# Attention and channel-mixing kernel: wider score banks, the mean read from its bank, the sums of P by two copies

## The chip, the cores and the metric

The kernel runs on one core of a Trainium2 chip. The metric is the device time of one execution in microseconds (us); every figure "ns" or "us" below comes from the times or the profile of this kernel. Engines: TensorE (PE in the profile; PEld is its weight load), VectorE (DVE), ScalarE (ACT), GpSimd (POOL), SyncE (SP, which issues most DMAs).

## The reference, cut to what matters

```python
# q, k, v: (8, 8, 576, 64); s: (8, 8, 576)
scores = (q @ k.T) / sqrt(64)
cum = cumsum(maximum(s, 0))
bias = -(cum[..., :, None] - cum[..., None, :])
scores = where(causal, -1e9, scores + minimum(bias, 0))
scores = scores - max(scores)
attn = exp(scores); attn = attn / (sum(attn) + 1e-9)
x = (attn @ v), heads side by side            # (8, 576, 512)
mixed = real(fft(fft(x, axis=1), axis=2))
u = x + mixed
un = (u - mean(u)) / sqrt(mean((u - mean(u))**2) + 1e-6)
out = u + maximum(un @ w_ch1, 0) @ w_ch2      # 512 -> 2048 -> 512
```

## The kernel before, in words

The 64 heads are worked in 32 pairs (`pair`, two heads side by side on the partitions), four pairs to a batch; after each batch its Fourier transform runs as matmuls (`folds`, `fourier`); after the attention comes the two-layer network over nine tiles of 512 tokens. Of the network, the first two tiles and the weights' conversion are woven into the end of the attention and the last Fourier transform (`norm_flow`, `plain_flow`, `mlp`); the third tile's norm is also made by `norm_flow`; the other tiles run in `fast_tile` with `ln_tile`, at an even pace to the end.

For one pair: `high` and `low` round q and k and make the rests, `maxes` finds the largest score of each query (units of matmuls into "psm" banks, reduced on VectorE), `scores` makes P, `av` makes P times v and the sums of P, `copies` takes those out, `recip` and `finish` divide.

`scores`, for each head: the keys stand in five chunks `CH` of 128, 128, 128, 128 and 64 keys, each against the queries that may see it. Chunk 0 takes two banks of 256 and 320 columns, chunk 1 one of 448, chunk 2 one of 320, chunk 3 one of 256 (of which 192 are used) and chunk 4 one of 64: six banks of 512 columns at most, from a ring of three ("ps") that the Fourier transform and the network's first product also use. Each bank gets two matmuls, one of KQ by KQ (L684) and one of K1 by Q1 for the rests (L685), each with its own 128x128 weights, and then one exponential on ScalarE (L690) that writes P in SBUF. When the exponentials of chunks 0 to 3 are done, one GpSimd instruction (`select`, L709) clears the triangle of four blocks; chunk 4 has one of its own (L697). `av` waits for both.

`av` puts the sums of P (one32 as the weights, L748) into the same bank as the first 128 columns of P times v (L740): sums of queries 0 to 383 on partitions 0 to 63, columns 0 to 383, sums of queries 384 to 575 on partitions 64 to 127, columns 0 to 191, values in columns 384 to 511. `copies` takes them out by three ScalarE instructions: 64x384 and 64x192 with the bias tile `tiny` (1e-9) added (L772), and 128x128 (L776). Two DMAs then gather the sums to a 48x24 tile, `recip` takes the reciprocal on VectorE (L789) and sends it through DRAM to all partitions (rd, rb), and `finish` multiplies (L820, L824).

`norm_flow`, for the first three tiles: the mean comes out of a matmul with `ones` into a bank; ScalarE copies it to SBUF (L1197); VectorE subtracts it from the four quarters of u (L1202); ScalarE squares the quarters (L1209, L1212) and GpSimd adds the squares (L1214); a second matmul, a root (L1223) and a reciprocal (L1226) follow. The quarters without their mean are rounded on ScalarE (L1235), VectorE makes the rests (L1238), and the product with w_ch1 (L1396) needs them.

The order of the instructions on each engine is not left to a scheduler of the compiler. `Flow` plays the program through with a cost for each step and due times built from the numbers in `PR`, and emits the instructions in the order in which it places them; an engine then works through its list in that order. A change of a cost or of a number in `PR` can change the order on every engine up to the end of this part, at some 700 us.

## Time and profile before

| | us |
|---|---|
| median of 3 runs | 1318.52 (1315.52 to 1319.11) |
| profiled execution, its own time | 1313.49 |
| its span in the trace | 1311.8 |
| granted TensorE clock, mean over the span | 0.982 of full |

| engine | busy share of the span |
|---|---|
| TensorE, matmuls | 94% |
| TensorE, weight loads | 79% |
| VectorE | 59% |
| ScalarE | 46% |
| GpSimd | 42% |

The profiled execution lies 5.0 us under the median. A busy TensorE in the profile counts a matmul until its modelled end, so neighbouring matmuls overlap in it: its pace is read from the starts of consecutive matmuls. The row of a wait names the engine that was idle and what it had waited for.

### The profile page before, as it was taken

Reading aid. Unit: us, or ns where it says so; the run is one execution under the profiler, and the core shown is the slowest. Engines: PE = TensorE matmul, PEld = TensorE weight load, DVE = VectorE, ACT = ScalarE, POOL = GpSimd, SP = SyncE. Lnnn points to the kernel's source line nnn. Section 1 sums busy time; section 2 is a strip of 40 time slices with the busy share of each in tenths; the row PEclk is TensorE's granted clock in tenths of the full one; section 3 lists DMA queues with packets and bytes.
Section 4 is the critical chain, followed back from the end, with each engine's and each line's share of the span. In section 5 each row is a group of like instructions: output and inputs, shape, how many; then the busy total and the mean of one; then the engine's idle time right before and its main releaser. Section 6 shows DMA issues by size and latency. Waiting matters only on the chain.

```text
span 1311.8 us, 22882 instructions
## 1 busy us (share of the span) xinstructions
PE 1235.9 (94%) x8414; PEld 1031.7 (79%) x8414; DVE 780.0 (59%) x1440; ACT 607.2 (46%) x1388; POOL 551.0 (42%) x569
## 2 busy tenths in 40 slices
PE   3998889899999979899999999999999999999998
PEld 2766667677776757787788888899888988888987
DVE  6566776847678577839757865444454444535323
ACT  2876776667676563425333432333233333333221
POOL 9456676857758675528743502102021021120100
PEclk9999899999999999999999999999999999999999
DMA  8867675646666465277543335244353442533433
GB/s 192 226 183 208 179 204 171 196 118 182 175 167 175 107 210 196 76 245 233 185 152 130 114 121 174 96 145 151 103 173 119 137 154 96 171 118 122 147 102 113
DMA packets 120395, 205.61 MB, mean 157 GB/s; under 512 B 16537, under 2 KB 38457, under 8 KB 120283
## 3 DMA queue, kind: packets, MB, share of 16 engines
q1 hardware_dynamic: 117707, 200.96, 49.1%
q0 software_dynamic: 1712, 2.53, 1.1%
q8 instruction: 66, 1.08, 0.3%
q10 hardware_dynamic: 864, 0.67, 0.2%
q14 instruction: 46, 0.38, 0.1%
HBM read 148.44 MB, written 31.72 MB: 137 GB/s over the span
## 4 chain that ended last, share of the span: by engine, by line
PE 55%; DVE 8%; POOL 3%; issue 3%; DMA 2%; ACT 1%; SPq 0%; POOLq 0%; DVEq 0%; ACTq 0%
PE b L347 20%; PE acc L259 7%; PE acc L258 7%; PE acc L260 7%; PE h L1396 4%; DVE we L88 1%; PE acc L1378 1%; PE acc L1377 1%; PE acc L1379 1%; DVE we L85 1%; PE pav L733 1%; PE pz L926 1%; DVE wl L1087 1%; PE pav L748 1%; DMA w2l<-wD 1%
## 5 line engine op out<-in xcount | busy, mean ns | idle before, releaser
L305 POOL TENSOR_TENSOR w<-w,o 128x512 f32<-128x512 f32 x28 | 37.2, 1338 | 346.5 <-DVE o L301 307.0
L259 PE MATMUL acc<-zh,w2l 128*128 128x512 f32 x452 | 179.3, 397 | 0.0
L258 PE MATMUL acc<-zh,w2h 128*128 128x512 f32 x452 | 178.8, 396 | 0.0
L260 PE MATMUL acc<-zl,w2h 128*128 128x512 f32 x452 | 177.2, 392 | 0.0
L690 ACT ACTIVATE P<-ps 128x320 f32<-128x320 f32 (+4 forms) x384 | 130.1, 393 | 41.3 <-PE ps L685 35.1
L684 PE MATMUL ps<-KQ 128*128 128x256 f32 (+3 forms) x384 | 121.9, 330 | 6.9 <-ACT P L690 6.3
L339 ACT ACTIVATE zh<-cs 128x256 fp32r<-128x256 f32 x112 | 58.8, 525 | 141.6 <-DVE cs L359 86.0
L685 PE MATMUL ps<-Q,K 128*128 128x256 f32 (+3 forms) x384 | 114.9, 312 | 0.0
L340 DVE SCALAR_TENSOR_TENSOR zl<-cs,zh 128x256 fp32r<-128x256 f32 x112 | 66.0, 590 | 69.2 <-ACT zh L339 69.2
L603 DVE CUSTOM_DVE_ANT_0 trash<-pm,amask 128x384 bf16<-128x384 f32 (+1 forms) x128 | 79.1, 618 | 39.4 <-PE pm L600 33.0
L554 POOL TENSOR_TENSOR Q<-qk,Q 64x576 fp32r<-64x576 f32 x64 | 95.2, 1508 | 17.1 <-DMA Q<-KQ 7.5
L347 PEld LDWEIGHTS b<-bh,wh 128*128 128x128 f32 x448 | 83.8, 188 | 22.0 <-DVE cs L359 2.4
L260 PEld LDWEIGHTS acc<-zl,w2h 128*128 128x128 f32 x452 | 85.0, 188 | 19.3 <-DVE zl L340 0.4
L347 PE MATMUL b<-bh,wh 128*128 128x256 f32 x448 | 89.2, 280 | 1.6 <-DVE cs L359 1.6
L684 PEld LDWEIGHTS ps<-KQ 128*128 128x128 f32 x384 | 75.4, 196 | 19.0 <-ACT P L690 14.2
L347 PE MATMUL b<-bh,wl 128*128 128x256 f32 x448 | 90.0, 282 | 0.0
L347 PE MATMUL b<-bl,wh 128*128 128x256 f32 x448 | 89.6, 281 | 0.0
L259 PEld LDWEIGHTS acc<-zh,w2l 128*128 128x128 f32 x452 | 86.3, 191 | 2.6
L733 PE MATMUL pav<-P,va 128*64 128x448 f32 (+3 forms) x640 | 87.3, 419 | 0.0
L258 PEld LDWEIGHTS acc<-zh,w2h 128*128 128x128 f32 x452 | 84.8, 188 | 2.9
L359 DVE TENSOR_TENSOR cs<-cs,b 128x256 f32<-128x256 f32 x56 | 23.5, 420 | 103.9 <-PE b L347 103.2
L733 PEld LDWEIGHTS pav<-P,va 128*64 128x64 f32 x640 | 43.2, 137 | 49.0 <-issue 39.8
(223 smaller groups left out, 3114.3 us busy)
## 6 DMA issues: line engine op xcount, KB each, us to landing
w2h<-w2D SPq DMA_DIRECT2D x128, 256.0 KB
w2l<-w2D SPq DMA_DIRECT2D x128, 256.0 KB
qk<-in_qkT_dram SPq DMA_DIRECT2D x32, 576.0 KB
raw<-in_wP_dram SPq DMA_DIRECT2D x32, 512.0 KB
va<-in_vA_dram SPq DMA_DIRECT2D x32, 320.0 KB
u<-uD SPq DMA_DIRECT2D x10, 1024.0 KB
Q<-KQ SPq DMA_DIRECT2D x32, 288.0 KB
K<-KQ SPq DMA_DIRECT2D x32, 288.0 KB
```

What stands on the lines that cost most here:

```text
L258: nc.tensor.matmul(acc[j], a[:, cs], y, start=first, stop=False)
L259: nc.tensor.matmul(acc[j], b[:, cs], y, start=False, stop=False)
L260: nc.tensor.matmul(acc[j], a[:, cs], z, start=False, stop=final)
L339: nc.scalar.activation(y[0][:, at], src, AF.Relu)
L340: nc.vector.scalar_tensor_tensor(out=y[1][:, at], in0=src, scalar=0.0, in1=y[0][:, at].bitcast(F32), op0=ALU.max, op1=ALU.subtract)
L347: nc.tensor.matmul(p[:, 0:256], a[:, j * 128:(j + 1) * 128], b[:, j], start=start and i == 0, stop=i == 5, skip_group_check=not start)
L554: nc.gpsimd.tensor_sub(q1[64:128, h], qk[0:64, h], q1[0:64, h].bitcast(F32))
L603: nc.vector.tensor_tensor_reduce(out=trash[:, 0:n], in0=p[:, 0:n], in1=amask[:, m0:m0 + n], scale=1.0, scalar=NEG, op0=ALU.add, op1=ALU.ma ...
L684: nc.tensor.matmul(p[:, :n], ky[:, h, ksl], qy[:, h, a:a + n], start=True, stop=False)
L685: nc.tensor.matmul(p[:, :n], k1[:, h, ksl], q1[:, h, a:a + n], start=False, stop=True)
L690: nc.scalar.activation(P[:, o:o + a + n - lo], p[:, lo - a:n], AF.Exp, scale=0.125)
L733: nc.tensor.matmul(p[64 * h:64 * h + 64, 0:n], va[:, c, 64 * h:64 * h + 64], P[h][:, o:o + n], start=start, stop=stop)
```

## The change

Four things change in what the kernel does, and the numbers in `PR` with them.

1. Scores take four banks a head: chunk 0's first 512 columns; its last 64 with chunk 1's 448; chunk 2's 320; chunk 3's 192 with chunk 4's 64. In a bank with two pieces there are four matmuls, so there are still twelve to a head. There is one exponential to a bank, and `select` waits for all four.
2. The first unit of `maxes` computes 128 columns a head and not 256.
3. The sums of queries 384 to 575 go to columns 192 to 383 of their bank; two ScalarE copies of 128x320 and 64x192 take sums and values out, without `tiny`; the 1e-9 is added on VectorE ahead of the reciprocal.
4. In `norm_flow` the mean is not copied: VectorE subtracts it from its bank; the squares are added on VectorE.

Of the numbers in `PR` nearly all are other ones; among them `T` goes from 14.85 to 14.86, `sel` 7.33 to 5.72, `av` 10.36 to 12.41, `lw` 41.24 to 50.68, `kp` 22.34 to 7.87, `dw` 8.84 to 4.43, `c0` 22.43 to 26.95, `fo2` 37.01 to 40.62, `fo3` 43.31 to 47.59.

```diff
-    tiny = const.tile([128, 1], F32, name="tiny")
-    nc.gpsimd.memset(tiny, 1e-9)
...
+            n = 256 if cut is None else cut + 128
...
-                nc.tensor.matmul(both[:, h], qy[:, h, 128 * c:128 * c + 128], ky[:, h, k0:k0 + 256], start=not h, stop=cut is None and h == 1, skip_group_check=True)
+                nc.tensor.matmul(both[:, h, 0:n], qy[:, h, 128 * c:128 * c + 128], ky[:, h, k0:k0 + n], start=not h, stop=cut is None and h == 1, skip_group_check=True)
...
-            def one(h, c, a, n, P, diag):
-                nk, q0, nq, qk = CH[c]
-                ksl = slice(128 * c, 128 * c + 128)
-                e, hold = yield pe(2 * mm(max(n, 128)), ring=(ring("ps", 3), 1))
+            def one(h, parts, P, diag):
+                total = sum(n for _, _, n in parts)
+                e, hold = yield pe(2 * sum(max(0.075, mm(n)) for _, _, n in parts), ring=(ring("ps", 3), 1))
                 p = bank("ps")
-                nc.tensor.matmul(p[:, :n], ky[:, h, ksl], qy[:, h, a:a + n], start=True, stop=False)
-                nc.tensor.matmul(p[:, :n], k1[:, h, ksl], q1[:, h, a:a + n], start=False, stop=True)
+                for x, (kk, qq) in enumerate(((ky, qy), (k1, q1))):
+                    o = 0
+                    for y, (c, a, n) in enumerate(parts):
+                        nc.tensor.matmul(p[:, o:o + n], kk[:, h, 128 * c:128 * c + 128], qq[:, h, a:a + n], start=x == y == 0, stop=x == 1, skip_group_check=True)
+                        o += n
...
-                e = yield act(a + n - lo, e)
-                nc.scalar.activation(P[:, o:o + a + n - lo], p[:, lo - a:n], AF.Exp, scale=0.125)
+                e = yield act(total, e)
+                nc.scalar.activation(P[:, o:o + total], p[:, 0:total], AF.Exp, scale=0.125)
...
+            for x, parts in enumerate((((0, 0, 512),), ((0, 512, 64), (1, 128, 448)), ((2, 256, 320),), ((3, 384, 192), (4, 512, 64)))):
+                flow.add(one(h, parts, P, diag), D(i) + PR['sc'] + PR['sch'] * h + PR['scs'] * 1.5 * x)
...
-                    nc.tensor.matmul(p[r:r + 32, a - 384 * t:a - 384 * t + n], one32, P[h][:, o:o + n], start=False, stop=k == 4, skip_group_check=True)
+                    nc.tensor.matmul(p[r:r + 32, a - 192 * t:a - 192 * t + n], one32, P[h][:, o:o + n], start=False, stop=k == 4, skip_group_check=True)
...
-            nc.scalar.activation(x[64 * t:64 * t + 64, 0:n], p[64 * t:64 * t + 64, 0:n], AF.Identity, bias=tiny[64 * t:64 * t + 64])
...
-        nc.scalar.copy(x[:, 384:512], p[:, 384:512])
+        nc.scalar.copy(x[:, 192:512], p[:, 192:512])
...
+        nc.scalar.copy(x[0:64, 0:192], p[0:64, 0:192])
...
+        nc.vector.tensor_scalar(sums, sums, 1e-9, None, op0=ALU.add)
         nc.vector.reciprocal(sums, sums)
...
-        mu, hmu = yield from tmp("mu")
-        e = yield act(512, e)
-        nc.scalar.copy(mu, pm)
...
-            nc.vector.tensor_sub(u[:, j], u[:, j], mu)
+            nc.vector.tensor_sub(u[:, j], u[:, j], pm)
...
-            e = yield pool_(512, e)
-            nc.gpsimd.tensor_add(t, t, t2)
+            e = yield dve(512, e)
+            nc.vector.tensor_add(t, t, t2)
```

## Rows read from the trace of the kernel before

**Rows 1.** The busy time of each engine by stage: stretch in us from the span's start, then busy us and instructions of TensorE, its weight loads, VectorE, ScalarE and GpSimd, the granted TensorE clock, the DMA engines' busy share and GB/s.

```profile
core 0: us, PE busy (x) PEld busy (x) DVE busy (x) ACT busy (x) POOL busy (x), PEclk, DMA share, GB/s
32.00:460.00 428.00, 401.34 (x3564) 306.53 (x3565) 296.14 (x664) 302.71 (x739) 291.14 (x329) 0.97 0.63 177
480.00:500.00 20.00, 11.24 (x51) 9.10 (x50) 20.00 (x28) 12.97 (x25) 15.86 (x9) 0.81 0.62 211
520.00:540.00 20.00, 16.17 (x83) 13.48 (x81) 19.98 (x27) 12.31 (x26) 11.94 (x10) 1.00 0.53 171
600.00:620.00 20.00, 16.90 (x65) 13.10 (x65) 18.66 (x18) 11.05 (x21) 16.59 (x12) 0.91 0.88 292
680.00:700.00 20.00, 20.00 (x88) 16.22 (x87) 10.32 (x13) 6.72 (x13) 5.48 (x4) 1.00 0.31 105
760.00:1311.00 551.00, 545.41 (x3384) 489.44 (x3382) 247.93 (x449) 170.75 (x388) 65.20 (x50) 1.00 0.40 132
```

**Rows 2.** Who waited for whom between 40 and 472 us, by engine: the idle engine, the tile and line that waited, what it waited for, the total in us, how often, the longest.

```profile
PEld ps L684 <- ACT P L690: 13.8, 31, 2.0
PEld pav L740 <- POOL P L709: 7.5, 13, 0.9
PEld pm L600 <- DVE Mx L593: 5.4, 7, 2.8
ACT P L690 <- PE ps L685: 33.8, 60, 1.7
POOL P L709 <- ACT P L690: 12.7, 9, 3.3
POOL xr L824 <- DMA rb<-rd: 11.4, 5, 6.3
```

**Rows 3.** TensorE's matmuls in order of time within 250 to 256 us: start, duration, line, operation, shape.

```profile
251.06 0.28 PE L685 MATMUL ps<-Q,K 128*128 128x256 f32 x1
251.18 0.31 PE L684 MATMUL ps<-KQ 128*128 128x320 f32 x1
251.33 0.31 PE L685 MATMUL ps<-Q,K 128*128 128x320 f32 x1
251.47 0.36 PE L684 MATMUL ps<-KQ 128*128 128x448 f32 x1
251.68 0.37 PE L685 MATMUL ps<-Q,K 128*128 128x448 f32 x1
251.88 0.35 PE L684 MATMUL ps<-KQ 128*128 128x320 f32 x1
...
254.65 0.28 PE L685 MATMUL ps<-Q,K 128*128 128x256 f32 x1
254.76 0.20 PE L684 MATMUL ps<-KQ 128*128 128x64 f32 x1
254.79 0.28 PE L685 MATMUL ps<-Q,K 128*128 128x64 f32 x1
```

**Rows 4.** TensorE's weight loads in order of time, same stretch and columns.

```profile
250.83 0.19 PEld L684 LDWEIGHTS ps<-KQ 128*128 128x128 f32 x1
250.94 0.19 PEld L685 LDWEIGHTS ps<-Q,K 128*128 128x128 f32 x1
251.06 0.19 PEld L684 LDWEIGHTS ps<-KQ 128*128 128x128 f32 x1
251.18 0.19 PEld L685 LDWEIGHTS ps<-Q,K 128*128 128x128 f32 x1
251.33 0.19 PEld L684 LDWEIGHTS ps<-KQ 128*128 128x128 f32 x1
...
254.65 0.19 PEld L684 LDWEIGHTS ps<-KQ 128*128 128x128 f32 x1
254.77 0.19 PEld L685 LDWEIGHTS ps<-Q,K 128*128 128x128 f32 x1
```

**Rows 5.** Groups of ScalarE instructions between 32 and 472 us, shapes kept apart: line, operation, out<-in, shape, count, then busy us and mean ns of one, then the engine's idle time before them and what ended it.

```profile
L690 ACT ACTIVATE P<-ps 128x320 f32<-128x320 f32 x128 | 56.0, 437 | 12.9 <-PE ps L685 10.9 <-ACT mt L649 1.7
L690 ACT ACTIVATE P<-ps 128x448 f32<-128x448 f32 x64 | 34.9, 545 | 5.9 <-PE ps L685 5.6
L690 ACT ACTIVATE P<-ps 128x256 f32<-128x256 f32 x64 | 24.6, 385 | 10.3 <-PE ps L685 8.5 <-PE pm L600 0.9
L690 ACT ACTIVATE P<-ps 128x192 f32<-128x192 f32 x64 | 21.2, 331 | 7.3 <-PE ps L685 6.4 <-PE pm L624 0.8
L772 ACT ACTIVATE stage<-pav,tiny 64x384 f32<-64x384 f32 x31 | 17.8, 575 | 24.1 <-PE pav L748 19.2 <-POOL P L709 2.5 <-issue 1.3
L763 ACT COPY stage<-pav 128x448 f32<-128x448 f32 x31 | 16.4, 530 | 11.5 <-PE pav L733 11.2
L690 ACT ACTIVATE P<-ps 128x64 f32<-128x64 f32 x64 | 14.3, 224 | 5.0 <-PE ps L685 3.8 <-PE pm L600 0.8
L772 ACT ACTIVATE stage<-pav,tiny 64x192 f32<-64x192 f32 x31 | 12.9, 417 | 0.8
L776 ACT COPY stage<-pav 128x128 f32<-128x128 f32 x31 | 8.2, 266 | 0.7
```

**Rows 6.** The same view for VectorE, two small instructions.

```profile
L789 DVE RECIPROCAL sums<-sums 48x24 f32<-48x24 f32 x30 | 8.6, 288 | 1.6 <-DMA sums<-stage 1.5
L950 DVE CAST z<-zc 96x1 fp32r<-96x1 f32 x24 | 2.3, 138 | 0.0
```

**Rows 7.** The same view for all engines between 470 and 720 us: the norm's instructions, and a product whose one input is a bank (L1309).

```profile
L1214 POOL TENSOR_TENSOR t<-t,t 128x512 f32<-128x512 f32 x9 | 15.3, 1700 | 13.6 <-ACT t L1212 13.6
L1309 DVE TENSOR_TENSOR o<-r,acc 128x512 f32<-128x512 f32 x12 | 8.1, 684 | 9.7 <-DMA w2h<-w2D 5.4 <-PE acc L1379 3.5 <-POOL o L1337 0.8
L1197 ACT COPY mu<-mu 128x512 f32<-128x512 f32 x3 | 1.8, 587 | 1.9 <-PE mu L1170 1.9
```

**Rows 8.** The subtractions of the mean (L1202): count, shortest, median and longest in ns, first and last start in us, shape.

```profile
L1202 DVE TENSOR_TENSOR u<-u,mu x12: 676/686/1885, 480.0 to 680.7; 128x512 f32<-128x512 f32 x12
```

**Rows 9.** VectorE in order of time between 478 and 540 us, from the stretches 478 to 500 and 519 to 540: start, duration, line, operation, shape, count, and idle time before with what ended it.

```profile
479.98 6.61 DVE L1202 TENSOR_TENSOR u<-u,mu 128x512 f32<-128x512 f32 x4 [0.75 <-ACT mu L1197]
...
487.60 0.68 DVE L1238 TENSOR_TENSOR bl<-u,bh 128x512 fp32r<-128x512 f32 x1
...
492.41 3.28 DVE L1238 TENSOR_TENSOR bl<-u,bh 128x512 fp32r<-128x512 f32 x2
...
521.28 0.68 DVE L1202 TENSOR_TENSOR u<-u,mu 128x512 f32<-128x512 f32 x1
```

More of the change, by code (lines that the diff above doesn't have):

```diff
@@ L581, in unit @@
         def unit(c, k0, cut, out, done):
-            e, hold = yield pe(2 * mm(256) + (0.0 if cut is None else 0.25), *ready[0], *ready[1], ring=(ring("psm", 3), 1))
+            n = 256 if cut is None else cut + 128
+            e, hold = yield pe(2 * mm(n) + (0.0 if cut is None else 0.25), *ready[0], *ready[1], ring=(ring("psm", 3), 1))
             p = psm.tile([128, 512], F32, tag="m", name="pm", bufs=3)
@@ L670, in scores @@
         st["P"], st["Phold"] = [], []
[L671 removed]
+        scored = Last(ev("scored", i), 8)
         for h in range(2):
@@ L698, in one @@
                     ev("P5", i, h).set(e)
-            x = 0
-            for c, (nk, q0, nq, qk) in enumerate(CH):
-                for a, n in [(0, 256), (256, 320)] if c == 0 else [(q0, nq)]:
-                    flow.add(one(h, c, a, n, P, diag), D(i) + PR['sc'] + PR['sch'] * h + PR['scs'] * x)
-                    x += 1
+            for x, parts in enumerate((((0, 0, 512),), ((0, 512, 64), (1, 128, 448)), ((2, 256, 320),), ((3, 384, 192), (4, 512, 64)))):
+                flow.add(one(h, parts, P, diag), D(i) + PR['sc'] + PR['sch'] * h + PR['scs'] * 1.5 * x)
             def select(P, diag, h):
@@ L736, in av @@
                  ((2, 256, 128), (3, 384, 192)))
-        e, phold = yield pe(mm4(128) + sum(0.02 + mm4(k[1][2]) for k in STEPS[:2]), ev("va", i), ring=(ring("psv", 2), 3))
+        e, phold = yield pe(mm4(128) + sum(0.02 + mm4(k[1][2]) for k in STEPS[:2]), ev("va", i), ring=(ring("psv", 2), 2))
         p = psm.tile([128, 512], F32, tag="v", name="pav", bufs=2)
@@ L768, in copies @@
         e0 = e
[L769 to L776 removed]
+        e1 = yield act(320, e0)
+        nc.scalar.copy(x[:, 192:512], p[:, 192:512])
+        phold.add(e1)
+        stored.add(e1)
+        e = yield act(192, e0)
+        nc.scalar.copy(x[0:64, 0:192], p[0:64, 0:192])
         phold.add(e)
[L778 to L781 removed]
+        for t, n, e in ((1, 192, e1), (0, 384, e)):
+            e = yield dma(3, e)
+            nc.sync.dma_start(out=sums[32 * t:32 * t + n // 12], in_=x[64 * t:64 * t + 64:32, 192 * t:192 * t + n])
             summed.add(e)
```

31 lines of the change are left out of this document (9 added, 22 removed).

## The prediction, made before the changed kernel was run

> **What bounds the kernel now.** I read the stages first, then the waits, then the single lines. The stages [rows 1] show three regimes. From 760 us to the end TensorE is busy 545 of 551 us; that part is made by `fast_tile`, which the change leaves alone, so its time stays. From 32 to 460 us, the attention, TensorE is busy 401 of 428 us, but VectorE, ScalarE, GpSimd and the DMA engines all stand at 63 to 71%: no engine is far from the others, and TensorE's busy time contains waiting. In the passage to the network VectorE is the full one: 20.00 of 20 us at 480 to 500 and 19.98 at 520 to 540, while TensorE has 11.2 and 16.2. What the change is worth must come from these last two regimes.
>
> In the attention the waits [rows 2] say what TensorE stands for: a score bank whose exponential isn't done costs its weight loader 13.8 us in 31 waits, `av` waits 7.5 us for `select`, and `select` in turn waits 12.7 us for exponentials. In the other direction ScalarE waits 33.8 us for scores. So a head's scores are a handover in which now one side is late and now the other.
>
> **Scores on TensorE.** The starts of matmuls in an unbroken stretch [rows 3] give the pace: 256 columns 0.12 us, 320 columns 0.15, 448 columns 0.20 to 0.21, that is 0.00045 us a column, so 512 columns 0.235. A 64-column matmul lasts 0.20 where a 256-column one lasts 0.28: 192 columns fewer take 0.08 less, so a narrow matmul isn't slower by the column, and one of 192 columns would stream in 0.09. But a new weight load follows no sooner than 0.11 us after the last [rows 4], and it begins when the matmul before it begins (251.18 and 251.33 in both groups). A matmul with fewer than 256 columns or so therefore takes 0.11. For one head before, two matmuls each: 256 (0.12), 320 (0.15), 448 (0.205), 320 (0.15), 256 (0.12), 64 (0.11): 2 x 0.855 = 1.71 us. After: 512 (0.235), 64 (0.11), 448 (0.205), 320 (0.15), 192 (0.11), 64 (0.11): 2 x 0.92 = 1.84. That is 0.13 to 0.14 us more a head though 64 columns fewer are computed, and 64 heads make 8.5 to 9 us more of TensorE's time; I take 9. The bounds: with 192 columns at the price of 256 (0.12) it is 10, with the two 64s hidden behind longer neighbours 2.
>
> The Trainium skill has a rule for each side of this on the page "TensorE: Matmul & The Clock Gate". Its section "Back-to-back issue gap" gives a small matmul little beyond its columns, by which 64 columns less would save, as an estimate, 0.05 us a head and 3.4 us in all. Its section "LDWEIGHTS (loading the stationary operand)" sets a load by its columns, 107 ns for 128, whatever the matmul behind it; the trace agrees with this second one (0.11).
>
> How much of the 9 us reaches the end depends on how often TensorE is what the others wait for. Its busy share is 94% [rows 1], with waits inside; between the 0.7 of its neighbours and 0.94 I take 0.85: **+7.8 us**.
>
> **Exponentials on ScalarE.** The widths give 0.83 ns a column ((545 - 385) / 192) [rows 5], so 512 columns cost 598 ns (bounds 545, the 448 row, and 770, two of 256). A head before: 385 + 437 + 545 + 437 + 331 + 224 = 2.36 us; after: 598 + 598 + 437 + 385 = 2.02 us. Saved 0.34 us a head, 22 us of ScalarE's time in all. Against TensorE's 1.71 us a head ScalarE was behind by 0.65; now against 1.84 by 0.18. The ring of three banks also holds up to 1,536 of a head's 1,600 columns, where it held 3 of 6 banks. I let the 13.8 us of TensorE's waits shrink with the lag, to 0.18 / 0.65 = 28%: **-10 us** (bounds 0, where the waits are set by other work in ScalarE's list, and -13.8). The last exponential of a head comes up to 0.34 us sooner, and `select` and `av` behind it: 13 waits of `av` by 0.15 to 0.34 is **-2 us** (bounds 0 and -4.4).
>
> **Sums of P.** Three instructions of 575 + 417 + 266 = 1.26 us a pair [rows 5] become a 128x320 copy (530 less 128 columns, 0.42) and a 64x192 one without the bias (0.32): 0.52 us less, 16.5 us of ScalarE in all. No wait of TensorE names these copies, so directly they give nothing; but with the exponentials ScalarE loses 38 us of its 303 in this stage, and everything that stands in its list behind (rounding q and k, the Fourier splits, the moved maxima) comes earlier. I take **-2 us** (0 to -5). VectorE gets one 48x24 addition a pair: between 138 ns (a one-column cast) and 288 (the reciprocal of that tile) [rows 6], taken 0.16, 5 us in all. It lies between the landed sums and the rd and rb transfers, and GpSimd waits for rb already 11.4 us in 5 waits [rows 2]; 5 x 0.16 is about **+0.5 us**. Cover: VectorE has 30% free here; without it, 5.
>
> **The maxima.** Two matmuls a pair go from 0.12 to the load's 0.11: 0.6 us in all, left out. VectorE's reduction behind it keeps its width.
>
> **The mean and the squares.** Only three tiles go this way; the subtractions of the first start at 480 us, of the second at 521 and of the third end at 681 [rows 8, 9]. For the first [rows 9] the four subtractions take 6.61 us, 1.65 each, while the second tile's take 0.68. A product with one input in a bank takes 684 ns as a mean of twelve [rows 7], also in crowded stretches. So reading the mean from its bank makes 6.6 us into 2.7, and the copy's 0.59 us [rows 7] is gone ahead of it: the centred tile is ready some 4.5 us earlier, in a stretch where VectorE is full and TensorE has nine idle microseconds. Against it nine additions come to VectorE from GpSimd (1.70 us each there), two thirds of them in full stretches; on VectorE each costs 0.68 if undisturbed and 1.65 if it meets GpSimd. First tile: -3.9 for the subtractions, +3 x 1.1 for the additions, and three long GpSimd instructions fewer to hold up the four L1238 (487.60 to 495.7) behind them, about -3: net -3.5. Second tile: nothing gained on subtractions, +3 x 0.7 to 1.1, less the copy: +1. Third tile: TensorE is busy 20.00 of 20 us and VectorE half free [rows 1]: nothing. Together **-2.5 us** (bounds -7 and +6).
>
> For this the Trainium skill, page "SBUF — State Buffer", section "Who interferes with whom", says that a VectorE instruction with two SBUF inputs and a GpSimd one that reads SBUF exclude each other, and one with an input in PSUM is free of it. The trace fits (1.65 against 0.68 on one line); by that rule alone the moved additions would speak against the change.
>
> **The sum.** +7.8 - 10 - 2 - 2 + 0.5 - 2.5 = -8.2 us, made against the profiled execution's own 1313.5 us: 1305.3. The runs' median lies 5.0 us above that execution, so on the scale of the runs 1310.3, and I say 1310.
>
> **The rivals.**
> *The weight loads decide (slower).* The 13.8 us may be waits of a TensorE that came early only to wait for something else next: its waits for maxima (5.4 us on L593) and for `select` stay as they are, and a head's scores are longer by 0.13 us. If less than 7.8 us of all waits goes, the change loses. With none gone and the passage at zero: 1318.5 + 7.8 to 9, about 1327. For it: every engine is at 63 to 71%, so no single relief need shorten anything. Against it: the lag of ScalarE in a head falls by more than twice what TensorE gains.
> *The lock of VectorE and GpSimd (slower).* Six moved additions in full stretches each meet a GpSimd instruction, 6 x 1.65 = 10 us on VectorE, less 4 from the subtractions, and the passage gets 6 us longer instead of 2.5 shorter: 1310 + 8.5, about 1319, no visible change.
> *Hidden anyway (no change).* Relief and loads cancel; the pace of the pairs is held by VectorE, GpSimd and transfers, which hardly change: about 1318.
> *ScalarE was the hub (faster by more).* All 13.8 us and 7.5 us of waits go, ScalarE's lighter list gives 5, the passage 7: 1318.5 + 7.8 - 33, about 1293.
> Across all of them lies the new order from the numbers in `PR`: clock dips such as the 0.81 at 480 to 500 and 0.91 at 600 to 620 [rows 1] cost 2 to 4 us apiece and may move or vanish; I count 5 us either way.
>
> **How the numbers follow.** The forecast has 0.40 (its own range 1303 to 1316), the hub 0.16, hidden 0.12, the lock 0.12, the weight loads 0.20. Within 0.3%, 1314.6 to 1322.5, is what a measurement of this kernel can hardly tell from no change. Faster: the hub, and most of the forecast, 0.16 + 0.36 = 0.52; same: 0.04 of the forecast, hidden 0.10, the lock 0.07, a little of the loads 0.03, 0.24; slower: 0.24. A range that leaves out the far half of the hub and the far half of the weight loads, 2 in 10 together, is 1295 to 1326.
>
> **What would show it.** In the changed profile: 256 exponentials with about 598 ns for 512 columns; 64- and 192-column matmuls at 0.11 us each; waits of score matmuls for exponentials at 4 us instead of 13.8; four subtractions of 0.68 us in the first tile, and the first L1396 earlier than the rest of the passage. I am wrong if the attention ends no sooner though those waits are gone, if additions of 1.65 us stand ahead of L1238, or if TensorE's loader has new waits for VectorE or GpSimd.

## The result and the profile after

The changed kernel takes 1323.22 us (median of 8 runs, 1318.42 to 1327.02) against 1316.26 of the kernel before on the same chip (8 runs, 1312.92 to 1319.11): ratio 1.0051, 95% interval 1.0031 to 1.0071. It is slower by half a per cent; 1310 and a gain had been predicted. Its profiled execution took 1318.42 us, 4.8 under its median; the one before took 1313.49, 2.8 under the 1316.26 of these eight runs. The two traces lie 4.9 us apart where the medians lie 7.0 apart.

Where the time went is read from three lines of the source in each kernel, each by its first and last start. Of the kernel before: the product P times v (the end of the attention), the network's first product, and the product of `fast_tile` (columns as in [rows 8]; shapes last).

```profile
L733 PE MATMUL pav<-P,va x640: 219/432/1009, 41.6 to 477.0; 128*64 128x448 f32 x64, 128*64 128x320 f32 x32, 128*64 128x192 f32 x32, 128*64 128x64 f32 x32
L1396 PE MATMUL h<-bh,wh x128: 389/394/632, 492.5 to 698.0; 128*128 128x512 f32 x128
L347 PE MATMUL b<-bh,wh x448: 274/279/388, 701.4 to 1298.1; 128*128 128x256 f32 x150
```

The same of the changed kernel:

```profile
L732 PE MATMUL pav<-P,va x640: 219/432/1010, 42.6 to 497.2; 128*64 128x448 f32 x64, 128*64 128x320 f32 x32, 128*64 128x192 f32 x32, 128*64 128x64 f32 x32
L1389 PE MATMUL h<-bh,wh x128: 388/392/632, 510.5 to 707.1; 128*128 128x512 f32 x128
L345 PE MATMUL b<-bh,wh x448: 274/279/388, 710.5 to 1302.8; 128*128 128x256 f32 x150
```

The attention ends 20.2 us later (497.2 against 477.0; five more traces with the order of before, of experiments below, have 479.2 to 481.4, so 477.0 is an early one). The gap to the network's first product shrinks from 15.5 to 13.3, the stretch from there to `fast_tile` from 208.9 to 200.0, and `fast_tile`, in which not one instruction was changed, from 596.7 to 592.3. So 20.2 are lost, 2.2 + 8.9 + 4.4 = 15.5 are won, and the span is 4.9 us longer. Two of these four stretches came out unforeseen: a loss in the attention where a gain was expected, and a gain in the untouched part.

The stages of the changed kernel (columns of [rows 1]):

```profile
32.00:490.00 458.00, 418.77 (x3664) 316.60 (x3664) 313.38 (x705) 283.39 (x607) 300.38 (x340) 0.97 0.62 171
490.00:510.00 20.00, 12.95 (x105) 8.51 (x105) 13.70 (x23) 12.83 (x29) 9.63 (x9) 0.89 0.61 192
510.00:530.00 20.00, 20.00 (x91) 17.35 (x92) 13.62 (x23) 4.75 (x9) 13.15 (x11) 0.85 0.59 176
```

How long TensorE stood in the attention is read from 40 us to the last start of P times v, before and then after (same columns):

```profile
40.00:477.00 437.00, 409.96 (x3696) 310.42 (x3697) 304.20 (x674) 307.05 (x753) 302.00 (x339) 0.98 0.62 176
```

```profile
40.00:497.20 457.20, 417.81 (x3699) 313.82 (x3699) 314.83 (x705) 279.31 (x599) 303.34 (x342) 0.96 0.61 169
```

TensorE is busy for 7.8 us more and idle for 39.4 us where it was idle for 27.0: of the later end 12.4 us are idle time of TensorE.

Its waits between 40 and 490 us (columns of [rows 2]):

```profile
POOL P L699 <- ACT P L693: 50.3, 21, 6.4
ACT P L693 <- PE ps L687: 34.8, 49, 3.6
PEld pav L739 <- POOL P L708: 14.2, 10, 4.7
PEld ps L687 <- ACT P L693: 2.5, 5, 0.7
```

Set against [rows 2], the wait that the prediction worked on did go: score banks not yet read cost the weight loader 2.5 us and no longer 13.8. But `av` now waits 14.2 us for `select`, before 7.5, and GpSimd's instruction for chunk 4 (L699), which stands in the list ahead of other GpSimd work, waits 50.3 us for exponentials. ScalarE waits for scores as long as before, 34.8 against 33.8. Of these two waits of TensorE, 13.8 + 7.5 = 21.3 us, 16.7 are left.

ScalarE's groups between 32 and 490 us (columns of [rows 5]), and two of VectorE's:

```profile
L693 ACT ACTIVATE P<-ps 128x512 f32<-128x512 f32 x128 | 75.0, 597 | 32.3 <-PE ps L687 28.9 <-PE pm L599 0.9
L769 ACT COPY stage<-pav 128x320 f32<-128x320 f32 x31 | 13.2, 425 | 51.9 <-PE pav L747 31.7 <-issue 14.7 <-DMA rb<-rd 2.9
L773 ACT COPY stage<-pav 64x192 f32<-64x192 f32 x31 | 9.7, 312 | 0.0
L785 DVE TENSOR_SCALAR sums<-sums 48x24 f32<-48x24 f32 x31 | 9.2, 297 | 5.4 <-DMA sums<-stage 3.4 <-issue 1.9
L786 DVE RECIPROCAL sums<-sums 48x24 f32<-48x24 f32 x31 | 9.1, 295 | 1.1
```

The durations are those that the prediction worked out: 597 ns for 512 columns (598), 425 and 312 for the two copies (420 and 320). Much of what ScalarE saved goes into standing ahead of the copy L769: 51.9 us of idle time, where its predecessor in [rows 5] has 24.1.

TensorE's matmuls in order of time, from 241 to 243.6 us. A pass is the matmuls of one bank with one pair of operands (KQ, or Q and K); a row with x2 joins the two pieces of a pass under the shape of the first, so only the passes' starts are read:

```profile
241.42 0.39 PE L687 MATMUL ps<-Q,K 128*128 128x512 f32 x1
241.65 0.48 PE L687 MATMUL ps<-KQ 128*128 128x64 f32 x2
241.97 0.47 PE L687 MATMUL ps<-Q,K 128*128 128x64 f32 x2
...
242.96 0.39 PE L687 MATMUL ps<-KQ 128*128 128x192 f32 x2
243.18 0.39 PE L687 MATMUL ps<-Q,K 128*128 128x192 f32 x2
243.41 0.42 PE L599 MATMUL pm<-KQ 128*128 128x384 f32 x1
```

A pass of 64 and 448 columns takes 0.32 us (0.11 + 0.205 by the prediction) and one of 192 and 64 takes 0.22 (0.11 + 0.11). By the pass, narrow matmuls cost what was priced, a weight load each.

### The profile page after: what moved, and what is told of

Same layout as the page of the kernel before. It is cut to its first block, busy times and chain, and to the rows that moved or that the text cites. A ratio compares the mean times of both kernels' runs of the same rounds, so it can differ in the third digit from the quotient of the medians.

```text
span 1316.7 us, 22716 instructions
## 1 busy us (share of the span) xinstructions
PE 1234.8 (94%) x8414; PEld 1029.4 (78%) x8414; DVE 788.9 (60%) x1481; ACT 576.2 (44%) x1225; POOL 536.6 (41%) x559
## 4 chain that ended last, share of the span: by engine, by line
PE 69%; DVE 7%; POOL 3%; DMA 3%; issue 3%; ACT 2%; SPq 1%; POOLq 0%; DVEq 0%; ACTq 0%
PE b L345 20%; PE acc L256 8%; PE acc L257 8%; PE acc L258 8%; PE h L1389 5%; PE ps L687 4%; PE pav L732 3%; PE pav L747 2%; PE pz L923 2%; PE acc L1371 1%; PE acc L1372 1%; PE acc L1370 1%; DVE we L86 1%; DVE we L83 1%; PE py L970 1%
## 5 line engine op out<-in xcount | busy, mean ns | idle before, releaser
L693 ACT ACTIVATE P<-ps 128x512 f32<-128x512 f32 (+2 forms) x256 | 119.7, 504 | 44.7 <-PE ps L687 37.4
L552 POOL TENSOR_TENSOR Q<-qk,Q 64x576 fp32r<-64x576 f32 x64 | 98.9, 1563 | 17.0 <-DMA Q<-KQ 14.4
L687 PE MATMUL ps<-KQ 128*128 128x64 f32 (+4 forms) x384 | 104.2, 327 | 1.8 <-ACT P L693 1.3
L687 PE MATMUL ps<-Q,K 128*128 128x64 f32 (+4 forms) x384 | 101.5, 322 | 0.0
L732 PEld LDWEIGHTS pav<-P,va 128*64 128x64 f32 x640 | 43.8, 140 | 51.9 <-issue 42.6
L687 PEld LDWEIGHTS ps<-KQ 128*128 128x128 f32 x384 | 70.7, 194 | 11.2 <-ACT P L693 2.5
```

The costliest lines, as they stand in the source:

```text
L552: nc.gpsimd.tensor_sub(q1[64:128, h], qk[0:64, h], q1[0:64, h].bitcast(F32))
L687: nc.tensor.matmul(p[:, o:o + n], kk[:, h, 128 * c:128 * c + 128], qq[:, h, a:a + n], start=x == y == 0, stop=x == 1, skip_group_check=True)
L693: nc.scalar.activation(P[:, o:o + total], p[:, 0:total], AF.Exp, scale=0.125)
L732: nc.tensor.matmul(p[64 * h:64 * h + 64, 0:n], va[:, c, 64 * h:64 * h + 64], P[h][:, o:o + n], start=start, stop=stop)
```

## The experiments

The theory after the result: narrow matmuls cost TensorE what was priced, fewer exponentials give back much less than was priced, and the rest is a matter of the new order and of small terms. Its rivals: the new numbers in `PR` alone make the loss; the squares on VectorE do; the 1e-9 addition on the way to the reciprocal does. All times are medians; a difference between two experiments is of their medians, and where its uncertainty is given, it is worked out from the two 95% intervals.

### The numbers and the scores, each alone

e1_old_numbers is the changed kernel with the numbers of before, e2_new_numbers the kernel before with the new numbers (the diff of e2, cut; e1's is the reverse).

```diff
...
-      'lw': 41.24, 'kp': 22.34, 'dw': 8.84,
+      'lw': 50.68, 'kp': 7.87, 'dw': 4.43,
...
```

> The changed kernel with the numbers in PR of the kernel before. Theory A, the narrow pieces of the score banks each cost a weight load on TensorE (some 0.17 us a head, 10 us in all), whatever the order: the attention still ends 10 us or more later than before (478 us there), time 1322 to 1330. Theory B, the new numbers made a worse order: the attention ends within 5 us of before, time 1308 to 1318.

> The kernel before with only the numbers in PR of the changed one. Theory A (weight loads): within 4 us of before, 1312 to 1320. Theory B (the numbers): 1323 or more, and the attention ends some 15 us later than before.

Measured: e1 1343.93, ratio 1.0209 (1.0170 to 1.0248); e2 1330.89, ratio 1.0115 (1.0082 to 1.0147).

e3_scores_only is the kernel before with the four-bank `scores` under the old numbers, e4_scores_undone the changed kernel with the old `scores` under the new ones.

```diff
-            def one(h, c, a, n, P, diag):
+            def one(h, parts, P, diag):
...
-                    flow.add(one(h, c, a, n, P, diag), D(i) + PR['sc'] + PR['sch'] * h + PR['scs'] * x)
+                flow.add(one(h, parts, P, diag), D(i) + PR['sc'] + PR['sch'] * h + PR['scs'] * 1.5 * x)
```

> The kernel before with only its scores in four banks, old numbers in PR. Theory A: the attention ends 10 us or more later, time 1323 to 1330. Theory B: at most 5 us of that, 1312 to 1320.

> The changed kernel with the scores of the kernel before (six banks a head), new numbers in PR. Theory A: the attention ends some 10 us sooner than in the changed kernel (497.5 us there), time 1308 to 1315. Theory B: no better than the changed kernel, 1320 to 1328.

Measured: e3 1344.01, ratio 1.0210 (1.0175 to 1.0245); e4 1326.56, ratio 1.0081 (1.0055 to 1.0108).

| | old numbers | new numbers |
|---|---|---|
| all as before | 1316.3 | 1330.9 |
| only the scores changed | 1344.0 | not run |
| all but the scores changed | not run | 1326.6 |
| all changed | 1343.9 | 1323.2 |

e1 and e3 are slower than either theory had expected; e2 and e4 came as the theory of the numbers had it. Neither the numbers nor the scores can be priced from this alone: the new scores cost 28 us under the old numbers and give 3 under the new, which is within the uncertainty of 4.4. e1 and e3 agree within 0.1 us, so under the old numbers all that is not scores comes to nothing on balance, though one gain is in it (`fast_tile` takes 592.0 us in e1 and 596.4 in e3). Each set of numbers does best with its own scores.

Two of these traces bear on the prediction. In e3, between 40 and 517 us, where its attention ends, TensorE's waits for exponentials and for `select` come to 12.5 us (21.3 before [rows 2]), and yet e3 is 28 us slower:

```profile
PEld pav L740 <- POOL P L709: 9.9, 9, 3.3
PEld ps L688 <- ACT P L694: 2.6, 7, 0.6
```

And in e2, which has the old scores, P times v ends at 498.1 us, as late as in the changed kernel, and TensorE is idle for 38.5 us until then (27.0 before, 39.4 in the changed kernel):

```profile
40.00:498.10 458.10, 419.59 (x3694) 316.58 (x3685) 305.13 (x676) 308.98 (x757) 305.73 (x340) 0.96 0.60 168
```

So a new order alone can make the attention end as late as it does in the changed kernel. The tests that follow therefore keep the order of every engine, and change only the instructions in it; only e12, e14 and e18 are about the order.

### Narrow matmuls

e5_split_448 is the kernel before, same order, with each score matmul of 448 columns cut into 64 and 384.

```diff
-                nc.tensor.matmul(p[:, :n], ky[:, h, ksl], qy[:, h, a:a + n], start=True, stop=False)
-                nc.tensor.matmul(p[:, :n], k1[:, h, ksl], q1[:, h, a:a + n], start=False, stop=True)
+                cuts = [(0, 64), (64, n)] if n == 448 else [(0, n)]
+                for x, (kk, qq) in enumerate(((ky, qy), (k1, q1))):
+                    for lo, hi in cuts:
+                        nc.tensor.matmul(p[:, lo:hi], kk[:, h, ksl], qq[:, h, a + lo:a + hi], start=x == 0 and lo == 0, stop=x == 1, skip_group_check=True)
```

> The kernel before, same order on every engine: only the score matmuls of 448 columns are split into 64 and 384 columns with the same weights, twice a head. By the starts of matmuls this adds 0.13 to 0.17 us of TensorE a head, 8 to 11 us in all, the same as the four banks add, and nothing else. Theory A (the weight loads of narrow pieces are on the path): 1323 to 1328. Theory B (they are hidden, the order of the four-bank plan costs the time): 1314 to 1319.

Measured: 1324.25, ratio 1.0063 (1.0042 to 1.0085), 8.1 us over the kernel before in the same comparison (1316.13). By the prediction's prices the cut costs 2 x (0.11 + 0.175 - 0.205) = 0.16 us a head, 10 us of TensorE; 0.8 of it reaches the end. P times v ends 11.9 us later than in the trace of before, and 7.5 to 9.7 later than in the five other traces of that order:

```profile
L735 PE MATMUL pav<-P,va x640: 219/432/1009, 42.1 to 488.9; 128*64 128x448 f32 x64, 128*64 128x320 f32 x32, 128*64 128x192 f32 x32, 128*64 128x64 f32 x32
```

e6_one_weight is the changed kernel, same order, with one matmul for each bank and pass; it leaves out the right scores of chunk 0's last 64 columns and of chunk 4 (it computes other columns in their place).

```diff
-                    for y, (c, a, n) in enumerate(parts):
-                        nc.tensor.matmul(p[:, o:o + n], kk[:, h, 128 * c:128 * c + 128], qq[:, h, a:a + n], start=x == y == 0, stop=x == 1, skip_group_check=True)
-                        o += n
+                    c, a = {0: (0, 0), 1: (1, 64), 2: (2, 256), 3: (3, 320)}[max(y for y, _, _ in parts if y < 4)]
+                    nc.tensor.matmul(p[:, 0:total], kk[:, h, 128 * c:128 * c + 128], qq[:, h, a:a + total], start=x == 0, stop=x == 1)
```

> The changed kernel, same order on every engine: each score bank of two pieces is filled by one matmul a pass with one chunk's weights (512 and 256 columns), so eight matmuls a head and not twelve; this leaves out the scores of the pieces with 64 columns, computed with the wrong chunk of keys. TensorE has 0.32 us less a head, 20 us in all. Theory A: the attention ends 10 us or more sooner, 1305 to 1313. Theory B: 1318 to 1323.

Measured: 1312.96, ratio 0.9972 (0.9956 to 0.9988), 10.3 us under the changed kernel. In its trace P times v ends at 492.6 us, 4.6 sooner, where 10 or more had been expected. By the starts above it takes (0.32 - 0.235) + (0.22 - 0.12) = 0.185 us away from a head's two-piece banks in each pass, 24 us in 128 passes; 10.3 of it, with an uncertainty of 3.4, reaches the end. That narrow matmuls cost time is shown from both sides. How much of TensorE's time comes through differs: 0.8 in e5, 0.43 in e6. For the change's own 8.3 us (0.13 us a head) that is an estimate of 4 to 7 us.

### Exponentials

e7_exp_halves is the changed kernel, same order, with each exponential of 512 columns made as two of 256 (385 ns each), 22 us more of ScalarE's time.

```diff
-                nc.scalar.activation(P[:, o:o + total], p[:, 0:total], AF.Exp, scale=0.125)
+                for lo, hi in ((0, 256), (256, 512)) if total == 512 else ((0, total),):
+                    nc.scalar.activation(P[:, o + lo:o + hi], p[:, lo:hi], AF.Exp, scale=0.125)
```

> The changed kernel, same order on every engine: the exponentials of 512 columns are made by two instructions of 256, so six a head as before; ScalarE has 0.34 us more a head, 22 us in all. If the fewer exponentials were worth the 10 to 12 us of the prediction: 1331 to 1335. If ScalarE's time is hidden: 1322 to 1326.

Measured: 1326.50, ratio 1.0090 (1.0064 to 1.0117): 3.3 us over the changed kernel (5.1 by the ratios, with an uncertainty of 4.4). This prices, in the new order, the very time, 22 us, for whose removal the prediction had set 10 and 2 more for `select`; 12 lies beyond the uncertainty.

e16_four_in_place is the kernel before with its plan and numbers, in which the four banks are computed at the places of the old ones and the two places left over stay empty.

```diff
+    BANKS = {(0, 0): (), (0, 256): ((0, 0, 512),), (1, 128): ((0, 512, 64), (1, 128, 448)), (2, 256): ((2, 256, 320),),
+             (3, 320): ((3, 384, 192), (4, 512, 64)), (4, 512): ()}
```

> The kernel before, its plan and numbers as they are, but the scores go to the four banks of the changed kernel at the places of the old plan (the places of chunk 0's first bank and of chunk 4 issue nothing). Theory D, the four banks cost what was measured one by one (8 us for narrow pieces, 3 us back for fewer exponentials) and the rest of the change's loss is the new order: 1318 to 1324. Theory E, the four banks lose more by themselves (larger steps of the handover): 1326 or more.

Measured: 1323.03, ratio 1.0045 (1.0027 to 1.0063), 6.9 us over the kernel before (1316.16). Four banks instead of six, with nothing else changed and no new order, make the kernel slower, about as much as e5's narrow matmuls alone (8.1, with an uncertainty of 3.7 on the difference): in the old order the fewer exponentials gave back 5 us at the most. (Chunk 0's scores begin one place later in it than before; what that costs was not tried.) Its waits between 40 and 490 us, and TensorE's time to the last start of P times v:

```profile
PEld ps L692 <- ACT P L699: 6.9, 10, 1.5
PEld pav L749 <- POOL P L718: 11.5, 16, 1.4
PEld pm L600 <- DVE Mx L593: 6.4, 8, 2.7
PEld pm L600 <- DVE Mx L603: 3.7, 9, 0.7
POOL P L706 <- ACT P L699: 6.1, 7, 1.5
```

```profile
40.00:492.90 452.90, 421.46 (x3699) 316.56 (x3699) 306.34 (x674) 300.63 (x629) 305.02 (x340) 0.97 0.61 171
```

TensorE's wait for exponentials is halved, 13.8 to 6.9, and yet TensorE is idle for 31.4 us, in an execution 5.5 us over its median (27.0 before, 26.8 to 29.3 in five more traces of that order). What it met next was in part the maxima: its waits for them at L600 are 10.1 us, 5.7 to 8.3 in the six traces. Its wait for `select`, 11.5, lies within the 7.9 to 12.6 that those six have in the same window, so that growth isn't shown here. GpSimd's long wait at the instruction for chunk 4 isn't there (6.1), so it doesn't come with the four banks alone.

e17_five_in_place is e15 (below) with chunk 4 computed in chunk 3's bank at its place: five exponentials a head, the matmuls' widths as before except 192 for 256.

```diff
+    BANKS = {(0, 0): ((0, 0, 256),), (0, 256): ((0, 256, 320),), (1, 128): ((1, 128, 448),), (2, 256): ((2, 256, 320),),
+             (3, 320): ((3, 384, 192), (4, 512, 64)), (4, 512): ()}
```

> The kernel before with the tile of 1e-9 moved and the mean read from its bank (1309.0), and chunk 4's 64 columns put into chunk 3's bank at that bank's place: five exponentials a head, no matmul narrower than before but chunk 3's, 192 for 256 columns. ScalarE saves 11 us; at 3.3 us for 22 that is 1.7 us: 1305 to 1309. If the larger step delays the select: 1310 to 1315.

Measured: 1312.40, ratio 0.9967 (0.9950 to 0.9985); e15 has 1309.0. Some 170 ns of ScalarE a head are saved (331 + 224 - 385, by [rows 5]), 11 us in all, and no gain is seen: it is 3.4 us slower, at the edge of the uncertainty of 3.5, and no cause was found. The expected one, a later `select`, isn't in its trace (TensorE waits 8.6 us for it between 40 and 472 us, 9.1 in e15).

### The 1e-9 addition, the squares, the plan's price

e11_no_eps is the changed kernel, same order, without the addition of 1e-9 to the sums.

```diff
-        nc.vector.tensor_scalar(sums, sums, 1e-9, None, op0=ALU.add)
         nc.vector.reciprocal(sums, sums)
```

> The changed kernel, same order, without the addition of 1e-9 ahead of the reciprocal; this leaves that addition out of the sums. If the extra instruction on the way from the sums to the product costs what the prediction gave (0.5 us): 1321 to 1325. If that way holds the pace of the pairs: 1314 to 1319.

Measured: 1318.16, ratio 1.0014 (0.9996 to 1.0033): 5 us under the changed kernel by the medians, but with an uncertainty of 3.6, and 1.8 by the profiled executions (1318.42 and 1316.61). P times v ends at 495.7 instead of 497.2, which is within what traces of one order differ by. That it costs something is likely; how much between 1.4 and 8.6 stays open.

e10_squares_pool is the changed kernel, same plan, with the squares added on GpSimd again.

```diff
-            nc.vector.tensor_add(t, t, t2)
+            nc.gpsimd.tensor_add(t, t, t2)
```

> The changed kernel, same plan: the nine additions of squares are given back to GpSimd at the places where VectorE had them. If the moved additions lengthen the passage (the lock of VectorE and GpSimd): 3 to 6 us less than the changed kernel, 1317 to 1320. If they are harmless or a gain: 1322 to 1327, with the stretch from the first product of the network to the first of the last seven tiles no shorter than the 200 us of the changed kernel.

Measured: 1324.67, ratio 1.0074 (1.0042 to 1.0105), 1.4 us over the changed kernel, within the uncertainty of 4.9. No harm of the moved squares is seen: in the changed kernel the nine take some 684 ns each on VectorE, as long as a product with one input in a bank [rows 7] (columns of [rows 8]):

```profile
L1207 DVE TENSOR_TENSOR t<-t,t x9: 675/683/691, 503.3 to 693.6; 128x512 f32<-128x512 f32 x9
```

e14_true_price is the changed kernel with the plan told what a narrow matmul takes.

```diff
-                e, hold = yield pe(2 * sum(max(0.075, mm(n)) for _, _, n in parts), ring=(ring("ps", 3), 1))
+                e, hold = yield pe(2 * sum(max(0.115, mm(n)) for _, _, n in parts), ring=(ring("ps", 3), 1))
```

> The changed kernel, but its plan reckons a score matmul of 64 or 192 columns at 0.115 us, near the 0.11 of the trace, and not at 0.075 and 0.094. The instructions are the same, their order is made anew. If the wrong price made the plan run ahead of the chip (GpSimd's waits for exponentials, 45 us at L699): 1312 to 1319 and those waits under 25 us. If any new order costs, fitted numbers being worth more than a right price: 1328 to 1345.

Measured: 1329.43, ratio 1.0107 (1.0071 to 1.0143), 6.2 us slower than the changed kernel. GpSimd's long wait is much shorter:

```profile
POOL P L699 <- ACT P L693: 30.5, 19, 3.4
```

50.3 became 30.5, and the kernel lost time. That speaks against this wait, the largest new one in the profile, as what the 20 us of the attention hang on; the order is another one as well, so it isn't settled. A truer price gave a worse order; that the numbers were fitted to the other price is the likely reason, not a tested one.

### The order alone

e18_spacing is the kernel before with one due time changed: 'scs' 0.78 for 0.76. The instructions are the same, in another order.

```diff
-  'scs': 0.76,
+  'scs': 0.78,
```

> The kernel before with one number of PR moved enough to change the order (scs, the spacing of the score units' due times, 0.78 for 0.76); no instruction changes. If a plan whose numbers aren't fitted loses 10 us and more: 1325 to 1345. If small changes of order are worth a few us either way: 1312 to 1321.

Measured: 1325.03, ratio 1.0055 (1.0036 to 1.0073), 8.9 us over the kernel before, more than the 7.0 of the whole change. The 21 us between e3 and e16, the same four banks under the same numbers, are likewise the order that the plan made of them. e12_one_number is the kernel before with 'T' 14.86 for 14.85.

```diff
-  'T': 14.85,
+  'T': 14.86,
```

> The kernel before with one number of PR moved by a hair, T 14.86 for 14.85, which changes the order but no instruction. Theory C, the time of a plan that isn't fitted to its program scatters upward by 10 us and more: 1325 to 1345. If the order is forgiving: 1313 to 1320.

Measured: 1316.54, ratio 1.0001 (0.9981 to 1.0020). Against what was expected, the order came out the same on every engine, so it tested nothing of an order; it shows how well a comparison of equal kernels repeats.

### The untouched part and the mean

e8_tiny_moved is the kernel before, same order, with the 4-byte tile `tiny` allocated behind the others instead of ahead of them.

```diff
-    tiny = const.tile([128, 1], F32, name="tiny")
-    nc.gpsimd.memset(tiny, 1e-9)
...
+    tiny = attb.tile([128, 1], F32, name="tiny")
+    nc.gpsimd.memset(tiny, 1e-9)
```

> The kernel before, same order of work: only the tile of 1e-9 is taken from another pool, so that what is allocated behind it in the first pool lies at other addresses. The stretch of the last seven tiles takes 607 us in the kernels with that tile in its old place and 602.5 in those without it. If the place is the cause: that stretch takes 602 to 603 us and the time is 1311 to 1313; if the norm's missing mean tile is the cause: 607 and 1315 to 1318.

Measured: 1311.54, ratio 0.9961 (0.9946 to 0.9976), 4.6 us faster. The product of `fast_tile` in it:

```profile
L345 PE MATMUL b<-bh,wh x448: 274/279/386, 703.6 to 1295.8; 128*128 128x256 f32 x150
```

592.2 us from first to last start, like the changed kernel (592.3), where the kernel before has 596.7. In dropping `tiny` the change moved the tiles behind it on that side of SBUF by 32 bytes, and this is the gain in the untouched part. All the traces agree: in the seven kernels with `tiny` in its old place this stretch takes 596.1 to 597.0 us, in the eleven that don't have it there and have no pad, 592.0 to 592.8.

e15_tiny_mean is e8 with the mean subtracted from its bank, same order.

```diff
-        nc.scalar.copy(mu, pm)
...
-            nc.vector.tensor_sub(u[:, j], u[:, j], mu)
+            nc.vector.tensor_sub(u[:, j], u[:, j], pm)
```

> The kernel before with the tile of 1e-9 in its other place (1311.5 without more) and the mean subtracted from its bank, without the copy, all else in the same order. By the prediction's working the first tile's four subtractions take 2.7 us for 6.6 and the passage gets 2 to 4 us shorter: 1307 to 1310. If other work in VectorE's list takes the place: 1311 to 1312.

Measured: 1309.00, ratio 0.9944 (0.9924 to 0.9965), 2.5 us under e8, with an uncertainty of 3.3. It beats the kernel before by 8.2 us and the changed one by 14. The subtractions of the mean, first tile included, and the network's first product:

```profile
L1201 DVE TENSOR_TENSOR u<-u,mu x12: 671/680/687, 483.4 to 680.8; 128x512 f32<-128x512 f32 x12
L1395 PE MATMUL h<-bh,wh x128: 387/392/690, 493.6 to 698.5; 128*128 128x512 f32 x128
```

The longest subtraction takes 687 ns, where [rows 8] have 1885. P times v ends at 481.3 us in e15, so the gap to the network's first product is 12.3; it is 12.3 too in e17, e19 and e20, which read the mean from its bank as well, and 15.4 or 15.5 before and in e5, e8, e12 and e16, which don't. These traces show the gain where it was forecast, some 3 us. e19_pad_64 and e20_pad_96 are e15 with an unused tile of 64 and of 96 bytes ahead of the others, to see whether the place within 64 bytes decides (the diff of e19; e20 has 24 for 16).

```diff
+    pad = const.tile([128, 16], F32, name="pad")
+    nc.vector.memset(pad, 0.0)
```

> The kernel with the tile of 1e-9 moved and the mean read from its bank (1309.0), and a pad of 64 bytes behind the first pool's last tile: what the network's tiles of that side start at moves up by 64 bytes, to 32 bytes off a multiple of 64 as without the pad. If the address within 64 bytes sets the pace of the last seven tiles: they take 602 to 603 us as without the pad.

> The same with a pad of 96 bytes: the tiles start at multiples of 64, as in the kernel before. If the address within 64 bytes sets the pace: the last seven tiles take about 607 us, 4.5 us more than with 64 bytes. If the tile's size or place mattered in another way: any other difference.

Measured: e19 1315.14, ratio 0.9998 (0.9979 to 1.0016); e20 1309.06, ratio 0.9945 (0.9920 to 0.9971). The product of `fast_tile`, e19 first, then e20:

```profile
L347 PE MATMUL b<-bh,wh x448: 274/283/387, 703.2 to 1301.1; 128*128 128x256 f32 x150
```

```profile
L347 PE MATMUL b<-bh,wh x448: 277/280/387, 701.0 to 1293.7; 128*128 128x256 f32 x150
```

597.9 and 592.7 us. The place within 64 bytes isn't it, against what e19 and e20 were expected to show: 64 bytes more make the part slow and 96 don't. By the kernels' allocations the tiles of that side start at 32 (e15), 0 (e20), 64 (before) and 96 (e19) of 128 bytes: the first two are fast, the other two slow. These are four points; why it is so was not found.

## Why the prediction was wrong, step by step

| step | predicted, us | measured, us | by |
|---|---|---|---|
| narrow score matmuls | +7.8 | +8.1 for a like cut; 4 to 7 estimated for this one | e5, e6 |
| fewer exponentials | -10 | -3.3 (uncertainty 4.4) in the new order; four banks in the old, with the line above, +6.9 | e7, e16 |
| `select` and `av` sooner; ScalarE's lighter list | -2, -2 | not measured alone; the wait for `select` grew | [rows 2], waits after |
| 1e-9 on VectorE | +0.5 | +5 (1.4 to 8.6) | e11 |
| mean from its bank | part of -2.5 | -2.5 (some -3 in the traces) | e15 against e8 |
| squares on VectorE | part of -2.5 | harmless (-1.4, within noise) | e10 |
| place of the tiles | not seen | -4.6 | e8 |
| new order | 5 either way | +9 to +21 for orders not fitted; the changed kernel's own part not separated | e18, e2, e3 against e16 |

**The step that failed** is "I let the 13.8 us of TensorE's waits shrink with the lag", -10 us, and with it the -2 for `select`. It is the case that the prediction named as its own refutation: the attention ends no sooner though those waits are gone. Much else that it asked of the profile is there: 256 exponentials with 597 ns for 512 columns, narrow matmuls that cost 0.11 us by the pass, four short subtractions. The waits did shrink, to 2.5 us even, below the forecast 4. But TensorE only came to other waits: it is idle for 39.4 us of the attention in the changed kernel and for 31.4 in e16, where the order is kept, against 27.0 before. In the changed kernel `av` waits 14.2 us for `select`, the other sign of error that the prediction had named (new waits of TensorE's loader for GpSimd). A wait in the row of its releaser was taken for time to be had. The halved exponentials of e7 price it in the new order: 22 us of ScalarE are worth 3.3 at the end. In the old order e16 against e5 shows a gain of 5 at the most. With 3.3 in place of the 10 and of the 2 for `select`, the sum is +7.8 - 3.3 - 2 + 0.5 - 2.5 = +0.5 us, and +2.5 without the 2 for ScalarE's lighter list, which was not tried alone: no gain would have been forecast.

Redone from its rows, the sum has small slips, and none of them turns its sign: 0.13 us in 64 heads are 8.3, not 8.5 to 9; 9 x 0.85 is 7.7, not 7.8; with the 64s hidden (0.03 us each by the columns) the bound on TensorE's time is about -2 and not +2; the second tile's terms give +1.5 to +2.7, not +1. Of the two 64-column matmuls in [rows 3] one lasts 0.20 us, as it reads, the other 0.28.

**The rival that came** is the one of the weight loads, with its reason: the waits were those of a TensorE that met something else next. Its condition, "If less than 7.8 us of all waits goes, the change loses", was met, for TensorE's idle time in the attention grew. Its 1327 stood on the 1318.5 of three runs; on the 1316.3 of the eight it is 1324 to 1325, and the measured 1323.2 has in it the unforeseen gain of 4.6 in the untouched part. The lock of VectorE and GpSimd is not borne out by e10. That the new numbers make the loss is only half refuted. e16 has none of them and loses 6.9, but e2 has nothing else and loses 14.6. The two losses don't add up to the measured 7.0, so how that divides between banks and order was not separated.

**The 1e-9 addition** took 0.16 us where it ran alone (at 502.25), as assumed, and 297 ns as a mean of 31; 9.2 us of VectorE, not 5. It was costed by the five waits for `rb` that had been seen, but stands on every pair's way from the sums to the division; that this is why it costs more is argued, not shown.

**The passage.** The four subtractions of the first tile took 2.48 us where 2.7 were forecast and 6.61 stood before:

```profile
499.85 2.48 DVE L1195 TENSOR_TENSOR u<-u,mu 128x512 f32<-128x512 f32 x4
502.25 0.16 DVE L785 TENSOR_SCALAR sums<-sums 48x24 f32<-48x24 f32 x1
```

Mean and squares account for only part of the 11 us that the passage gained. From the network's first product to `fast_tile` it took 201.8 us in e10 (squares on GpSimd), 208.3 in e15 (mean alone), 208.4 in e16, 206.4 in e2, 206.1 in e4 (mean and squares, old scores), and 200.0 in the changed kernel. With the gap ahead of it (15.5 before, 11.8 in e2) the new numbers alone bring 6.2 of the 11 us: the larger part comes with the new order, which may leave less for this stretch and more for the attention.

**What stays open.** The measured terms, +6.9 + 5 - 4.6 - 2.5 - 1.4, make +3.4; the change measured +7.0. The rest, 3.6, is within the uncertainty of the terms. They were measured in two different orders, and what the changed kernel's order costs or gives back was not priced, so that the terms add up isn't shown. TensorE's granted clock doesn't tell it. Between 120 and 210 us, before and then after (columns of [rows 1]):

```profile
120.00:210.00 90.00, 78.73 (x667) 60.44 (x667) 68.42 (x137) 65.03 (x156) 67.21 (x71) 0.94 0.68 194
```

```profile
120.00:210.00 90.00, 78.64 (x658) 56.40 (x658) 69.52 (x133) 53.54 (x115) 66.18 (x66) 0.89 0.73 196
```

The mean is 0.94 of full (2.4 GHz) in the one and 0.89 in the other; as the clock has but two levels, 1.2 and 2.4 GHz, that is an estimated 11 and 20 of the 90 us at the lower one. Ahead of the longest such stretch in the changed kernel TensorE was busy for 6.55 of the 10 us from 140 to 150. But in the order of before e16 has 0.92 there and e17 0.89, and e6, in the new order, has 0.86 and is 10.3 us faster than the changed kernel; over the whole span both kernels have 0.982. What brings the clock down in this stretch was not tested. The two copies of the sums were not tried alone, nor the half of the first `maxes` unit.

## What to carry to other kernels

A wait that a profile lists is what the engine stood for last, not what it gains when the wait goes: before crediting a relief, look up what the same engine waits for next, and price it by an experiment that puts the work back in place (22 us of ScalarE were worth 3.3 us here). A narrow matmul with weights of its own cost a weight load here (0.11 us by the pass), and merging banks in the old order, which made matmuls narrower, lost 6.9 us. Where a planner writes the order, test an edit at the old places first: other due times alone cost this kernel 9 us (e18) and 15 (e2), more than the edit's 7.

## What the runs showed of the hardware

The place of the tiles in SBUF changed a steady stretch of TensorE by 0.8%: 592.2 us with the tiles of one side 32 bytes lower (e8), 596.7 before, with the same instructions in the same order, and a 64-byte pad made it slow again (597.9, e19). The median duration of the same matmul follows it in part: 283 ns in e19 against 279 in e15, but 279 also in the slow kernel before, so the cause isn't read from that line.

The Trainium skill, page "TensorE: Matmul & The Clock Gate", section "LDWEIGHTS (loading the stationary operand)", sets a load by its columns, 107 ns for 128; the starts in the changed kernel agree (0.32 us for a pass of 64 and 448 columns, 0.22 for one of 192 and 64). Its section "Back-to-back issue gap" has a formula by which a matmul takes little beyond its columns, but for an isolated matmul; of a stream in which each matmul has its own weight load, like this kernel's scores, the section says that both set the spacing and that the formula comes out too low at few columns. By the formula alone e5 would have changed next to nothing; its +8.1 us agree with what the section says of the stream.

VectorE took 684 ns as a mean for the nine additions of squares with both inputs in SBUF, in the changed kernel, where GpSimd was less busy (9.63 of 20 us at 490 to 510; 15.86 at 480 to 500 before [rows 1]); the 1.65 us a piece that [rows 9] show for the same kind of instruction didn't come back. In e10, with these additions on GpSimd (1379 ns each there), VectorE's twelve L1231, which have two inputs in SBUF as well, took 1012 ns as a mean, against 784 in the changed kernel.
